# Slot logits in four copies, slot sums by column groups, and 128 bytes of padding in SBUF

## The chip, the cores and the metric

One core of a Trainium2 chip runs the whole program. The metric is the device time of one execution in microseconds. The engines are TensorE (PE, with its weight loads shown apart as PEld), VectorE (DVE), ScalarE (ACT), GpSimd (POOL) and SyncE (SP); DMAs are issued here from GpSimd (inputs and weights) and from SyncE (output).

## What is computed

Sliding-window attention over q, k, v of 8 batches, 8 heads, 576 positions and 64 dimensions, then a soft mixture of experts over its result x of 4608 tokens and 512 columns:

```python
scores = q @ k.T / 8; mask: 0 <= row - col < 64; attn = softmax(scores) @ v
x = attn.transpose(0, 2, 1, 3).reshape(4608, 512)
logits = x @ phi                              # 4608 x 32 slots, 8 experts x 4
d = exp(logits - max over tokens); d /= d.sum(0)
slot_input = (d.T @ x).reshape(8, 4, 512)
slot_out[e] = relu(slot_input[e] @ w1[e]) @ w2[e]     # 512 -> 1024 -> 512
c = exp(logits - max over slots); c /= c.sum(1)
out = c @ slot_out                            # 4608 x 512
```

The kernel takes no maximum away before either exp. One exp of the logits therefore serves both d and c; they differ in the sum that they are divided by.

## The kernel before

The attention goes through 16 units, each one batch and four heads (half of the heads). A unit has three steps j. A step transposes windows of v (stage_t2), makes scores for four windows of 64 queries (one window in the third step) and takes their exp on ScalarE to the tile pm (stage_s), transposes q, k or v of the next unit (stage_t1, copies to SBUF mostly by ScalarE), and multiplies the pm of the step before by v (stage_av, whose result goes to x_bp). The scores have one PSUM buffer, the tiles named tr, lt, pa and te share four.

GpSimd issues all loads in the order in which they are written, and that order is kept by hand (manual_schedule). issue_loads(u) loads q, k and v of unit u + 3 into three rotating buffers and one quarter of an expert's weights (load_w, 512 KB in SBUF); at unit 13 all that is left of the weights is issued in one go. The last weight tile, w2l, lies in a buffer of x_bp. All loads turn float32 in HBM into float16 in SBUF. At most eight of them are under way at a time: each waits for the one eight places ahead to have landed.

When both halves of a batch are through, six further pieces of work follow, one appended to each of the next six steps (the list todo): stage_xt(b, 0), (b, 1) and (b, 2) transpose x, chunk by chunk of 128 tokens (four chunks for even batches, five for odd ones, in which the last halves of two batches make up a chunk); stage_logit multiplies the transposed chunks by phi and takes the exp to ex, four copies side by side, with its sum over slots; stage_slot multiplies x by ex and adds up over batches in acc, a further product with ones giving the sum over tokens; stage_et transposes ex to ET. For the last batch all six follow the loop at once.

Then the experts: expert_h and expert_o work with four column groups of TensorE side by side, in each group a product with 32 slots. sop collects the result of all experts in one bank, slot_oa is its copy, and the last loop makes 36 products cp of ET with slot_oa, scales them by crcp and stores them by SyncE from the tiles ob, which lie in the buffers of w1s.

Of the kernel before, what the change touches and what calls it, by code (L numbers as in the profile page):

```python
# [8 lines left out]
FP32 = mybir.dt.float32  # L9
FP16 = mybir.dt.float16  # L10
AF = mybir.ActivationFunctionType
ALU = mybir.AluOpType
# [4 lines left out]
def kernel(  # L17
# [29 lines left out]
    pxt = ctx.enter_context(tc.tile_pool(name="pxt", bufs=3))  # L47
# [58 lines left out]
    ones = const.tile([128, 128], FP16, name="ones")  # L106
    nc.vector.memset(ones, 1.0)
# [15 lines left out]
    nc.gpsimd.dma_start(out=phi_sb, in_=moe_phi.rearrange("(c p) s -> p c s", p=128))  # L123

    ET = const.tile([128, 4 * B + B // 2, 128], FP16, name="ET")
    crcp = const.tile([128, B, 5], FP32, name="crcp")
    acc = const.tile([128, 5, NSLOT], FP32, name="acc")
# [122 lines left out]
    def stage_xt(b, part):  # L250
        xb = xbp[b // 2]
        ch = moe_chunks(b)[2 * part:2 * part + 2]
        if not ch:
            return
        tr = ps.tile([128, 8, 128], FP16, name="tr", tag="tr", bufs=4)
        for n, c in enumerate(ch):
            for kk in range(NHD):
                nc.tensor.transpose(tr[:, 4 * n + kk, :], xb[:, c, 128 * kk:128 * kk + 128], ident[:, :])  # L258
        xT = pxt.tile([128, 8, 128], FP16, name="xT", tag="xT")
        nc.vector.tensor_copy(out=xT[:, 0:4 * len(ch), :], in_=tr[:, 0:4 * len(ch), :])  # L260
        moe[b, part] = xT

    def stage_logit(b):
        ch = moe_chunks(b)
        lt = ps.tile([128, 5, NSLOT], FP32, name="lt", tag="tr", bufs=4)
        for n, c in enumerate(ch):
            xT = moe[b, n // 2]
            for kk in range(NHD):
                nc.tensor.matmul(lt[:, n, :], xT[:, 4 * (n % 2) + kk, :], phi_sb[:, kk, :],  # L269
                                 start=(kk == 0), stop=(kk == NHD - 1))  # L270
        nch = len(ch)
        ex = psm.tile([128, 5, 4, NSLOT], FP16, name="ex", tag="ex", bufs=2)
        nc.scalar.activation(ex[:, 0:nch, :, :],
                             lt[:, 0:nch, :].unsqueeze(2).broadcast_to([128, nch, 4, NSLOT]), AF.Exp)
        rs = psm.tile([128, 5], FP32, name="rs", tag="rs")
        nc.vector.reduce_sum(rs[:, 0:nch], ex[:, 0:nch, 0, :], axis=AXX)
# [3 lines left out]
    def stage_slot(b):  # L280
        ch = moe_chunks(b)
        xb = xbp[b // 2]
        ex = moe["ex", b]
        pa = ps.tile([128, 5, NSLOT], FP32, name="pa", tag="tr", bufs=4)
        for n, c in enumerate(ch):
            for dc in range(NHD + 1):
# [162 lines left out]
```

## Time and profile before

| what | value |
|---|---|
| median of 13 runs | 198.52 us (196.84 to 201.62) |
| the profiled execution | 197.24 us, of which the span from its first to its last instruction is 195.4 us |
| loads (q0) | 30.97 MB in SBUF, 94.2% of the span of 16 DMA engines |
| stores (q1) | 9.44 MB, 13.8% |
| TensorE | busy 142.1 us, 73% of the span |
| ScalarE, VectorE | busy 109.7 and 109.1 us, 56% each |
| HBM | 61.93 MB read, 9.44 MB written |

A row of a timeline has start, duration, engine, line, operation, out<-in and number of instructions, and in brackets the idle time before it and what ended it. A row of the chain has start, duration and what held the time. A row of a table of stages has the stretch, its length, busy time of PE, PEld, DVE, ACT and POOL (with number of instructions), the granted TensorE clock, the DMA engines' share and GB/s written. "issue" as a releaser means that nothing in the profile shows what the engine waited for. The profiled execution is one of the faster ones of the 13.

### The profile page before, as it was taken

To read this page: it belongs to the slowest core of one execution; us is meant where nothing else is said; L and a number is where in the kernel's file an instruction comes from. 1 tells how busy PE (TensorE), PEld (TensorE's weight loads), DVE (VectorE), ACT (ScalarE), POOL (GpSimd) and SP (SyncE) were. 2 spreads that over 40 slices of the span, in tenths; PEclk is the share of its full clock that TensorE was granted. 3 is DMA by queue.
4 is the path that set the end of the run, shared out by engine and by line. 5 is a ranking of instruction groups with operands and counts; after the bars stand their busy time and mean duration, and the time that the engine had idled before them with its cause. 6 is when DMAs were issued, how large, how long until landed. Compare 5 with 4: busy or idle time off the path is not lost.

```text
span 195.4 us, 7045 instructions
## 1 busy us (share of the span) xinstructions
PE 142.1 (73%) x3148; PEld 106.1 (54%) x3148; DVE 109.1 (56%) x268; ACT 109.7 (56%) x164; POOL 59.6 (31%) x89
## 2 busy tenths in 40 slices
PE   0699999878987879884988986898757774882000
PEld 0476777766766657763876865787644541220000
DVE  3026688657674757753885864578853113894000
ACT  2556876957566596765669566676311223893000
POOL 7953544434241424321442952232210000000000
PEclk9999999999999999999999998799985999798555
DMA  4999999999999999999699999999999991899995
GB/s 65 168 202 207 207 208 209 204 206 209 211 208 204 207 208 207 210 188 173 88 189 193 184 166 209 209 208 211 207 211 207 211 205 26 322 379 379 379 330 143
DMA packets 31310, 40.84 MB, mean 209 GB/s; under 512 B 2097, under 2 KB 22577, under 8 KB 31281
## 3 DMA queue, kind: packets, MB, share of 16 engines
q0 software_dynamic: 26384, 30.97, 94.2%
q1 hardware_dynamic: 4896, 9.44, 13.8%
q8 instruction: 24, 0.39, 0.7%
q14 instruction: 6, 0.04, 0.1%
HBM read 61.93 MB, written 9.44 MB: 365 GB/s over the span
## 4 chain that ended last, share of the span: by engine, by line
PE 43%; ACT 16%; DMA 13%; issue 10%; DVE 7%; POOL 1%; DVEq 0%; ACTq 0%; POOLq 0%
DMA w2l<-in_moe_w_dram 10%; PE tr L146 10%; PE tr L177 8%; ACT pm L200 7%; ACT kT L153 6%; PE sc L188 6%; PE sc L195 5%; PE av L223 4%; DVE ob L408 4%; DMA vn<-in_v_dram 3%; PE tr L258 2%; ACT qT L153 2%; PE cp L402 2%; PE pa L288 2%; PE lt L269 2%
## 5 line engine op out<-in xcount | busy, mean ns | idle before, releaser
L200 ACT ACTIVATE pm<-sc 128x1024 f16<-128x1024 f32 (+1 forms) x48 | 39.5, 822 | 38.6 <-PE sc L195 36.0
L178 DVE COPY vw<-tr 128x1024 f16<-128x1024 f16 (+1 forms) x48 | 26.5, 551 | 7.4 <-PE tr L177 7.3
L177 PE MATMUL tr<-ident,vT 128*128 128x128 f16 x288 | 24.8, 224 | 1.1 <-DVE rc L229 0.9
L153 ACT COPY qT<-tr 128x640 f16<-128x640 f16 (+1 forms) x32 | 21.9, 745 | 4.9 <-PE tr L146 4.9
L223 PE MATMUL av<-vw,pm 128*64 128x65 f16 x576 | 19.4, 197 | 4.2 <-issue 2.9
L231 DVE TENSOR_TENSOR x_bp<-av,rc 128x512 f16<-128x512 f32 x32 | 22.0, 688 | 0.8
L153 ACT COPY kT<-tr 128x640 f16<-128x640 f16 (+1 forms) x32 | 22.0, 761 | 0.2 <-PE tr L146 0.2
L188 PE MATMUL sc<-rep,hide 64*128 64x512 f16 (+1 forms) x96 | 20.8, 346 | 1.8 <-ACT pm L200 1.3
L195 PE MATMUL sc<-qT,kT 64*128 64x64 f16 x576 | 20.1, 193 | 1.9 <-issue 1.9
L177 PEld LDWEIGHTS <-vT 128*128 128x128 f16 x288 | 17.6, 100 | 4.7 <-issue 2.6
L195 PEld LDWEIGHTS <-kT 64*128 64x128 f16 x576 | 15.4, 96 | 7.3 <-issue 4.1
L223 PEld LDWEIGHTS <-pm 128*64 128x64 f16 x576 | 15.8, 112 | 6.6 <-issue 5.2
L61 POOL DMA_DIRECT2D vn<-in_v_dram x16 | 11.5, 717 | 21.1 <-PE av L223 16.8
L146 PE MATMUL tr<-ident,qn 128*64 128x128 f16 x288 | 12.3, 233 | 7.7 <-DMA qn<-in_q_dram 5.4
L151 DVE COPY vT<-tr 128x512 f16<-128x512 f16 x16 | 11.6, 726 | 10.9 <-PE tr L146 10.8
L61 POOL DMA_DIRECT2D qn<-in_q_dram x16 | 11.5, 717 | 18.5 <-PE av L223 10.4
L61 POOL DMA_DIRECT2D kn<-in_k_dram x16 | 11.5, 717 | 16.2 <-PE av L223 11.9
L81 POOL DMA_DIRECT2D w1s<-in_moe_w_dram x16 | 11.4, 718 | 13.4 <-DMA w1s<-in_moe_w_dram 9.9
L146 PE MATMUL tr<-ident,vn 128*64 128x128 f16 x288 | 13.4, 227 | 2.6 <-ACT kT L153 0.7
L146 PEld LDWEIGHTS <-qn 128*64 128x64 f16 x288 | 9.5, 117 | 8.6 <-DMA qn<-in_q_dram 5.4
L84 POOL DMA_DIRECT2D w2s<-in_moe_w_dram x14 | 10.6, 767 | 11.3 <-DMA w2s<-in_moe_w_dram 7.9
L408 DVE TENSOR_SCALAR ob<-cp,crcp 128x512 f32<-128x512 f32 x18 | 12.6, 747 | 1.3 <-PE cp L402 1.2
(63 smaller groups left out, 216.8 us busy)
## 6 DMA issues: line engine op xcount, KB each, us to landing
out_dram<-ob SPq DMA_DIRECT2D x18, 512.0 KB, 5.5
w1s<-in_moe_w_dram POOLq DMA_DIRECT2D x16, 512.0 KB, 13.6
w2s<-in_moe_w_dram POOLq DMA_DIRECT2D x14, 512.0 KB, 13.5
qn<-in_q_dram POOLq DMA_DIRECT2D x16, 288.0 KB, 10.6
kn<-in_k_dram POOLq DMA_DIRECT2D x16, 288.0 KB, 10.5
vn<-in_v_dram POOLq DMA_DIRECT2D x16, 288.0 KB, 9.9
w2l<-in_moe_w_dram POOLq DMA_DIRECT2D x2, 512.0 KB, 19.7
phi_sb<-in_moe_phi_dram POOLq DMA_DIRECT2D x1, 32.0 KB, 7.2
```

The costliest lines, as they stand in the source:

```text
L61: nc.gpsimd.dma_start(out=t, in_=src[b, 4 * half:4 * half + 4].rearrange("(x h) (g t) d -> (h g) x (t d)", x=2, h=2, t=T))
L146: nc.tensor.transpose(tr[64 * x:64 * x + 64, j, :], src[:, x, 64 * (t0 + j):64 * (t0 + j) + 64], ident[:, :])
L151: nc.vector.tensor_copy(out=o, in_=i)
L153: nc.scalar.copy(out=o, in_=i)
L177: nc.tensor.transpose(tr[:, 2 * w + h, :], st["vT"][:, h, 64 * i:64 * i + 128], ident[:, :])
L178: nc.vector.tensor_copy(out=st["vw"][:, wins[0]:wins[0] + n, :, 0:64], in_=tr[:, 0:2 * n, :].rearrange("p (w h) (x d) -> p w (h x) d", h=2 ...
L188: nc.tensor.matmul(sc[:, x, 0:128 * n], hide[64 * x:64 * x + 64, :], rep[64 * x:64 * x + 64, 0:2 * n, :], start=True, stop=False, skip_gro ...
L195: nc.tensor.matmul(sc[:, x, o:o + 64], st["kT"][64 * x:64 * x + 64, h, 64 * i:64 * i + 128], st["qT"][64 * x:64 * x + 64, h, 64 * i:64 * i ...
L200: nc.scalar.activation(pm[:, :, 0:2 * n, :], sc[:, :, 0:128 * n].rearrange("p x (w q) -> p x w q", q=64), AF.Exp, scale=scale)
L223: nc.tensor.matmul(av[r0:r0 + 64, kk, 65 * (w // 2):65 * (w // 2) + 65], pm[:, x, h * n + w, :], st["vw"][:, i, 2 * h + x, 0:65], start=Tr ...
L231: nc.vector.tensor_tensor(out=xb[:, c0:c0 + 2, 256 * half:256 * half + 256].rearrange("p c (k d) -> p k c d", d=64), in0=avv[:, :, :, 0:64 ...
L408: nc.vector.tensor_scalar(out=ob[:, g, :], in0=cp[:, :], scalar1=cr, scalar2=None, op0=ALU.mult)
```

## The change

Logits are made the other way round: phi, copied four times side by side (phi4), is the weight, and up to 512 tokens stream through, so that lt has slots on partitions, in four copies, and its exp is ET at once; ScalarE's instruction also writes the sum over tokens to esum. A fifth chunk takes four products of its own (l8) and an exp of its own. The new stage_ex multiplies ET by a part of the identity matrix, which gives ex with tokens on partitions; ScalarE copies it, VectorE takes the sum over slots. stage_slot takes ex as the weight, 32 columns in one of four column groups, and streams the 512 columns of x. Its four partial sums lie in four groups of partitions of pa; acc is now 128 x 512. After the loop acc is scaled by one over the sum over tokens (dinv) and sel4, a stack of four identity matrices, adds the four groups and transposes at once (si). The six pieces of work are now xt, xt, xt, logit, ex, slot. issue_loads takes two weight quarters in units 2, 5, 8 and 11. The pool of xT has one buffer of 4 KB and one of 1 KB, and a tile of 128 bytes (gap), which nothing uses, stands behind it in SBUF: the tiles w1s, w2s and ob start at 105056 and onward in steps of 8192 before, 104448 after (96 and 0 bytes past a multiple of 512), qn, kn and vn at 96 and 0 past a multiple of 256. TensorE's program has 5826 rows after, 6298 before.

```diff
@@ -44,7 +44,9 @@
     ppm = ctx.enter_context(tc.tile_pool(name="ppm", bufs=2))
     psm = ctx.enter_context(tc.tile_pool(name="psm", bufs=4))
     pxb = ctx.enter_context(tc.tile_pool(name="pxb", bufs=2))
-    pxt = ctx.enter_context(tc.tile_pool(name="pxt", bufs=3))
+    pxt = ctx.enter_context(tc.tile_pool(name="pxt", bufs=1))
+    gap = ctx.enter_context(tc.tile_pool(name="gap", bufs=1))
+    gap.tile([128, 64], FP16, name="gap")
     pw1 = ctx.enter_context(tc.tile_pool(name="pw1", bufs=8))
     pw2 = ctx.enter_context(tc.tile_pool(name="pw2", bufs=7))
     pet = ctx.enter_context(tc.tile_pool(name="pet", bufs=2))
@@ -103,8 +105,10 @@
         nc.vector.tensor_copy(
             out=rep[64 * h:64 * h + 64, :, :],
             in_=ident[64 * h:64 * h + 64, 64 * h:64 * h + 64].unsqueeze(1).broadcast_to([64, 8, 64]))
-    ones = const.tile([128, 128], FP16, name="ones")
-    nc.vector.memset(ones, 1.0)
+
+    sel4 = const.tile([128, NSLOT], FP16, name="sel4")
+    with nc.allow_low_precision("sums of 0 and 1"):
+        nc.vector.reduce_sum(sel4, ident.rearrange("p (g s) -> p s g", s=NSLOT), axis=AXX)
     kTs, vTs, vws, hTs = [], [], [], []
     for n in range(2):
         kt = const.tile([128, 2, 64 + S], FP16, name=f"kT{n}")
@@ -121,10 +125,13 @@
         vws.append(vw)
     phi_sb = const.tile([128, NHD, NSLOT], FP16, name="phi_sb")
     nc.gpsimd.dma_start(out=phi_sb, in_=moe_phi.rearrange("(c p) s -> p c s", p=128))
+    phi4 = const.tile([128, NHD, 4, NSLOT], FP16, name="phi4")
+    nc.vector.tensor_copy(out=phi4, in_=phi_sb.unsqueeze(2).broadcast_to([128, NHD, 4, NSLOT]))
 
     ET = const.tile([128, 4 * B + B // 2, 128], FP16, name="ET")
     crcp = const.tile([128, B, 5], FP32, name="crcp")
-    acc = const.tile([128, 5, NSLOT], FP32, name="acc")
+    acc = const.tile([128, D], FP32, name="acc")
+    esum = const.tile([128, B + B // 2], FP32, name="esum")
     slot_inT = const.tile([128, NHD, NSLOT], FP16, name="slot_inT")
     slot_oa = const.tile([128, D], FP16, name="slot_oa")
     for n in range(2):
@@ -252,56 +259,66 @@
         ch = moe_chunks(b)[2 * part:2 * part + 2]
         if not ch:
             return
+        nch = len(ch)
+        if part == 0:
+            moe[b] = pxt.tile([128, NHD, 4, 128], FP16, name="xT", tag="xT")
         tr = ps.tile([128, 8, 128], FP16, name="tr", tag="tr", bufs=4)
+        for kk in range(NHD):
+            for n, c in enumerate(ch):
+                nc.tensor.transpose(tr[:, nch * kk + n, :], xb[:, c, 128 * kk:128 * kk + 128], ident[:, :])
+        if part < 2:
+            nc.vector.tensor_copy(out=moe[b][:, :, 2 * part:2 * part + 2, :],
+                                  in_=tr[:, :, :].rearrange("p (k n) q -> p k n q", n=2))
+        else:
+            moe[b, 8] = pxt.tile([128, NHD, 128], FP16, name="xT8", tag="xT8")
+            nc.vector.tensor_copy(out=moe[b, 8], in_=tr[:, 0:4, :])
+
+    def stage_logit(b):
+
+        lt = ps.tile([128, 512], FP32, name="lt", tag="tr", bufs=4)
+        for kk in range(NHD):
+            nc.tensor.matmul(lt[:, :], phi4[:, kk].rearrange("p r s -> p (r s)"), moe[b][:, kk],
+                             start=(kk == 0), stop=(kk == NHD - 1))
+        nc.scalar.activation(ET[:, 4 * b:4 * b + 4, :], lt[:, :].rearrange("p (c q) -> p c q", q=128),
+                             AF.Exp, accum_out=esum[:, b:b + 1])
+        if b % 2:
+            l8 = ps.tile([128, 128], FP32, name="l8", tag="tr", bufs=4)
+            for kk in range(NHD):
+                nc.tensor.matmul(l8[:, :], phi4[:, kk].rearrange("p r s -> p (r s)"), moe[b, 8][:, kk],
+                                 start=(kk == 0), stop=(kk == NHD - 1))
+            nc.scalar.activation(ET[:, 4 * B + b // 2, :], l8[:, :], AF.Exp,
+                                 accum_out=esum[:, B + b // 2:B + b // 2 + 1])
+
+    def et_chunks(b):
+        return [4 * b + n for n in range(4)] + ([4 * B + b // 2] if b % 2 else [])
+
+    def stage_ex(b):
+
+        ch = et_chunks(b)
+        nch = len(ch)
+        te = ps.tile([128, 5, NSLOT], FP32, name="te", tag="tr", bufs=4)
         for n, c in enumerate(ch):
-            for kk in range(NHD):
-                nc.tensor.transpose(tr[:, 4 * n + kk, :], xb[:, c, 128 * kk:128 * kk + 128], ident[:, :])
-        xT = pxt.tile([128, 8, 128], FP16, name="xT", tag="xT")
-        nc.vector.tensor_copy(out=xT[:, 0:4 * len(ch), :], in_=tr[:, 0:4 * len(ch), :])
-        moe[b, part] = xT
-
-    def stage_logit(b):
-        ch = moe_chunks(b)
-        lt = ps.tile([128, 5, NSLOT], FP32, name="lt", tag="tr", bufs=4)
-        for n, c in enumerate(ch):
-            xT = moe[b, n // 2]
-            for kk in range(NHD):
-                nc.tensor.matmul(lt[:, n, :], xT[:, 4 * (n % 2) + kk, :], phi_sb[:, kk, :],
-                                 start=(kk == 0), stop=(kk == NHD - 1))
-        nch = len(ch)
-        ex = psm.tile([128, 5, 4, NSLOT], FP16, name="ex", tag="ex", bufs=2)
-        nc.scalar.activation(ex[:, 0:nch, :, :],
-                             lt[:, 0:nch, :].unsqueeze(2).broadcast_to([128, nch, 4, NSLOT]), AF.Exp)
+            nc.tensor.matmul(te[:, n, :], ET[:, c, :], ident[:, 0:NSLOT], start=True, stop=True)
+        ex = psm.tile([128, 5, NSLOT], FP16, name="ex", tag="ex", bufs=2)
+        nc.scalar.copy(out=ex[:, 0:nch, :], in_=te[:, 0:nch, :])
         rs = psm.tile([128, 5], FP32, name="rs", tag="rs")
-        nc.vector.reduce_sum(rs[:, 0:nch], ex[:, 0:nch, 0, :], axis=AXX)
+        nc.vector.reduce_sum(rs[:, 0:nch], te[:, 0:nch, :], axis=AXX)
         nc.vector.reciprocal(crcp[:, b, 0:nch], rs[:, 0:nch])
         moe["ex", b] = ex
 
     def stage_slot(b):
+
+        ex = moe["ex", b]
+        pa = ps.tile([128, D], FP32, name="pa", tag="tr", bufs=4)
         ch = moe_chunks(b)
-        xb = xbp[b // 2]
-        ex = moe["ex", b]
-        pa = ps.tile([128, 5, NSLOT], FP32, name="pa", tag="tr", bufs=4)
         for n, c in enumerate(ch):
-            for dc in range(NHD + 1):
-                lhs = xb[:, c, 128 * dc:128 * dc + 128] if dc < NHD else ones[:, :]
-                nc.tensor.matmul(pa[:, dc, :], lhs, ex[:, n, 0, :],
-                                 start=(n == 0 and dc == 0), stop=(n == len(ch) - 1 and dc == NHD),
-                                 skip_group_check=True)
+            g = n % 4
+            nc.tensor.matmul(pa[32 * g:32 * g + 32, :], ex[:, n, :], xbp[b // 2][:, c, :],
+                             start=(n < 4), stop=(n + 4 >= len(ch)), skip_group_check=True)
         if b == 0:
-            nc.vector.tensor_copy(out=acc[:, :, :], in_=pa[:, :, :])
-        else:
-            nc.vector.tensor_tensor(out=acc[:, :, :], in0=pa[:, :, :], in1=acc[:, :, :], op=ALU.add)
-
-    def stage_et(b):
-        ex = moe["ex", b]
-        nch = len(moe_chunks(b))
-        te = ps.tile([128, 8, 128], FP16, name="te", tag="tr", bufs=4)
-        for n in range(nch):
-            nc.tensor.transpose(te[:, n, :], ex[:, n].rearrange("p r s -> p (r s)"), ident[:, :])
-        nc.vector.tensor_copy(out=ET[:, 4 * b:4 * b + 4, :], in_=te[:, 0:4, :])
-        if nch > 4:
-            nc.vector.tensor_copy(out=ET[:, 4 * B + b // 2, :], in_=te[:, 4, :])
+            nc.vector.tensor_copy(out=acc[:, :], in_=pa[:, :])
+        else:
+            nc.vector.tensor_tensor(out=acc[:, :], in0=pa[:, :], in1=acc[:, :], op=ALU.add)
 
 
     nu = len(units)
@@ -310,7 +327,8 @@
     def issue_loads(u):
         if u + 3 < nu:
             load_unit(u + 3)
-            load_w(*w_order.pop(0))
+            for _ in range(2 if u % 3 == 2 else 1):
+                load_w(*w_order.pop(0))
 
     load_w(*w_order.pop(0))
     load_unit(2)
@@ -334,7 +352,7 @@
                 if pj == 2 and units[pu][1] == 1:
                     b = units[pu][0]
                     todo += [lambda b=b: stage_xt(b, 0), lambda b=b: stage_xt(b, 1), lambda b=b: stage_xt(b, 2),
-                             lambda b=b: stage_logit(b), lambda b=b: stage_slot(b), lambda b=b: stage_et(b)]
+                             lambda b=b: stage_logit(b), lambda b=b: stage_ex(b), lambda b=b: stage_slot(b)]
             pend = (u, j)
             if todo:
                 todo.pop(0)()
@@ -346,16 +364,23 @@
     stage_xt(b, 1)
     stage_xt(b, 2)
     stage_logit(b)
+    stage_ex(b)
     stage_slot(b)
-    stage_et(b)
+    dinv = const.tile([128, 2], FP32, name="dinv")
+    nc.vector.reduce_sum(dinv[:, 0:1], esum[:, :], axis=AXX)
+    nc.vector.reciprocal(dinv[:, 1:2], dinv[:, 0:1])
+
+    pa_sb = slot_oa
+    nc.scalar.activation(pa_sb[:, 0:256], acc[:, 0:256], AF.Copy, scale=dinv[:, 1:2])
+    nc.vector.tensor_scalar(out=pa_sb[:, 256:512], in0=acc[:, 256:512], scalar1=dinv[:, 1:2], scalar2=None, op0=ALU.mult)
     psum1.close()
 
 
     ps2 = ctx.enter_context(tc.tile_pool(name="ps2", bufs=2, space=bass.MemoryType.PSUM, reuse_waits="tile"))
-    dinv = const.tile([128, NSLOT], FP32, name="dinv")
-    nc.vector.reciprocal(dinv, acc[:, NHD, :])
-    nc.vector.tensor_tensor(out=slot_inT[:, :, :], in0=acc[:, 0:NHD, :],
-                            in1=dinv[:, :].unsqueeze(1).broadcast_to([128, NHD, NSLOT]), op=ALU.mult)
+    si = ps2.tile([128, NHD, NSLOT], FP32, name="si", tag="hp")
+    for dc in range(NHD):
+        nc.tensor.matmul(si[:, dc, :], pa_sb[:, 128 * dc:128 * dc + 128], sel4[:, :], start=True, stop=True)
+    nc.vector.tensor_copy(out=slot_inT, in_=si)
 
     sel = ident[:, :].rearrange("p (g s) -> p g s", s=NSLOT)
     sop = ps2.tile([128, D], FP32, name="sop", tag="sop", bufs=1)
```

Three places in the order of instructions.

GpSimd, the loads issued in unit 2 and the first of unit 3; before:

```order
L61 DMA qn<-in_q_dram 128x2x576
L61 DMA kn<-in_k_dram 128x2x576
L61 DMA vn<-in_v_dram 128x2x576
L84 DMA w2s<-in_moe_w_dram 128x4x512
L61 DMA qn<-in_q_dram 128x2x576
```

and after:

```order
L63 DMA qn<-in_q_dram 128x2x576
L63 DMA kn<-in_k_dram 128x2x576
L63 DMA vn<-in_v_dram 128x2x576
L86 DMA w2s<-in_moe_w_dram 128x4x512
L83 DMA w1s<-in_moe_w_dram 128x2x1024
L63 DMA qn<-in_q_dram 128x2x576
```

A second weight load stands ahead of the next unit's q.

ScalarE, the first two steps of a unit in which the logits of an odd batch (five chunks) are made; before:

```order
L153 COPY qT<-tr 128x128x4
L273 ACTIVATE ex<-lt 128x640
L200 ACTIVATE pm<-sc 128x1024
L153 COPY kT_116<-tr 128x2x64x5
L153 COPY kT_116<-tr 128x2x64x4
L200 ACTIVATE pm<-sc 128x2x128
```

and after:

```order
L160 COPY qT<-tr 128x128x4
L282 ACTIVATE ET,esum<-lt 128x512
L289 ACTIVATE ET,esum<-l_2253 128x128
L207 ACTIVATE pm<-sc 128x1024
L160 COPY kT_120<-tr 128x2x64x5
L160 COPY kT_120<-tr 128x2x64x4
L303 CAST ex<-te 128x160
L207 ACTIVATE pm<-sc 128x2x128
```

The exp is split in two and the copy of te comes ahead of the third step's exp.

VectorE, from the last transposes of x to the experts; before:

```order
L260 COPY xT<-tr 128x512
L276 TENSOR_REDUCE rs<-ex 128x5
L277 RECIPROCAL crcp<-rs 128x5
L294 TENSOR_TENSOR acc<-pa,acc 128x160
L302 COPY ET<-te 128x512
L304 COPY ET<-te 128x128
L356 RECIPROCAL dinv<-acc 128x32
L357 TENSOR_TENSOR slot_inT<-acc,dinv 128x128
```

and after:

```order
L274 COPY xT_3702<-tr 128x512
L370 TENSOR_REDUCE dinv<-esum 128x1
L371 RECIPROCAL dinv<-dinv 128x1
L305 TENSOR_REDUCE rs<-te 128x5
L306 RECIPROCAL crcp<-rs 128x5
L321 TENSOR_TENSOR acc<-pa,acc 128x512
L375 TENSOR_SCALAR slot_oa<-acc,dinv 128x256
L383 CAST slot_inT<-si 128x128
```

The copies to ET are gone, the sum is wider, and a scaling and the products si (on TensorE) lie between it and slot_inT.

## The prediction

> **What bounds the kernel now.** I read the page first (the slices, the DMA queues, the chain that ended last), then the DMA rate stage by stage, the end of the experts on TensorE, one step of the loop, and last the way from the loop to the experts and the stores.
>
> ```profile
> span 195.4 us, 7045 instructions
> ...
> q0 software_dynamic: 26384, 30.97, 94.2%
> q1 hardware_dynamic: 4896, 9.44, 13.8%
> q8 instruction: 24, 0.39, 0.7%
> ...
> PE 43%; ACT 16%; DMA 13%; issue 10%; DVE 7%; POOL 1%; DVEq 0%; ACTq 0%; POOLq 0%
> ```
>
> The loads (q0, 31 MB) and the stores (q1, 9.4 MB) share the 16 DMA engines, and the stores cannot start before the last expert is done. So the span is: loads and attention side by side, then the experts, then the stores. The stage view gives the DMA rate (last number of a row, GB/s) over three stretches.
>
> ```profile
> 15.00:85.00 70.00, 59.77 (x1532) 48.13 (x1530) 48.09 (x111) 48.84 (x73) 26.39 (x37) 1.00 1.20 207
> 85.00:118.00 33.00, 28.03 (x746) 23.23 (x740) 22.30 (x54) 23.51 (x35) 14.43 (x20) 1.00 1.07 169
> 118.00:161.00 43.00, 33.60 (x738) 24.60 (x735) 21.99 (x65) 18.22 (x30) 7.31 (x10) 0.88 1.18 208
> ```
>
> 207 to 208 GB/s is the full rate of the loads; between 85 and 118 us they ran at 169. The queue was empty there at times: 33 x (1 - 169/207) = 6.1 us of transfer were lost. The next rows say who was late (waiter, releaser, us in total, times, longest), and then how the experts ended.
>
> ```profile
> POOL vn L61 <- PE av L223: 16.8, 8, 4.0
> PE tr L146 <- DMA qn<-in_q_dram: 5.4, 1, 5.4
> ...
> 158.75 0.21 PE L374 MATMUL th<-ident,h_sb 128*128 128x16 f16 x2 [0.33 <-ACT h_sb L371]
> 158.89 0.40 PE L386 MATMUL sop<-w2s,hT 128*32 128x512 f16 x3
> ...
> 160.76 0.40 PE L386 MATMUL sop<-w2l,hT 128*32 128x512 f16 x4
> 163.09 0.40 PE L386 MATMUL sop<-w2l,hT 128*32 128x512 f16 x4 [1.93 <-DMA w2l<-in_moe_w_dram]
> ```
>
> GpSimd waits for TensorE to give input buffers back; TensorE waits for inputs only once, 5.4 us at the start. So the loop is a compute loop, and the DMA has a hole in it. At the end the two paths are nearly level: TensorE had everything else done at 161.16 (160.76 + 0.40) and waited 1.93 us for the last weights. That is all that a faster load can give, unless the compute path gets shorter too.
>
> **The loads.** Four more weight DMAs (512 KB, 2.5 us each at 208 GB/s) go into units 2, 5, 8 and 11, and as many leave the block at unit 13. Three of them, 7.5 us, are queued before or just as the hole opens, and it lost 6.1; so the last weights land about 163.0 - 6.1 = 157 and the wait of 1.93 us goes: **-1.9**. Less would be gained only if TensorE then came late for another reason, which stands in the terms below. The extra DMA stands in the queue behind its own unit's inputs and ahead of the next unit's, 2.5 us of delay. Since TensorE waits for inputs at the start alone, I cost that at nothing; its cover is three units of buffers, and without it each of the four would cost up to 2.5 us.
>
> **The loop.** Each step of a unit turns on ScalarE: exp of the scores (pm), copies of q or k, again exp. The rows are of one batch of five chunks: ScalarE and TensorE in order of time, the three removed TensorE stages from the chain, and three groups (busy us, mean ns) of small copies.
>
> ```profile
> 84.91 1.02 ACT L200 ACTIVATE pm<-sc 128x1024 f16<-128x1024 f32 x1 [2.62 <-PE sc L195]
> 85.83 1.37 ACT L153 COPY qT<-tr 128x640 f16<-128x640 f16 x2
> 87.04 0.73 ACT L273 ACTIVATE ex<-lt 128x640 f16<-128x640 f32 x1
> 87.62 1.06 ACT L200 ACTIVATE pm<-sc 128x1024 f16<-128x1024 f32 x1
> ...
> 86.77 0.40 PE L195 MATMUL sc<-qT,kT 64*128 64x64 f16 x16
> 91.35 0.19 PE L288 MATMUL pa<-ex,ones 128*128 128x32 f16 x1 [2.61 <-issue]
> ...
> 85.56 0.60 PE lt L269 x20
> 88.04 0.70 PE pa L288 x24
> 92.76 0.39 PE te L301 x5
> ...
> L371 ACT ACTIVATE h_sb<-hp 128x256 f16<-128x256 f32 x8 | 3.1, 384 | 12.0 <-PE hp L367 12.0
> L302 DVE COPY ET<-te 128x512 f16<-128x512 f16 x8 | 3.1, 392 | 0.4 <-PE te L301 0.4
> L304 DVE COPY ET<-te 128x128 f16<-128x128 f16 x4 | 0.9, 213 | 0.0
> ```
>
> Logit step: ScalarE runs without a gap from 84.91 to 87.62, while the scores that its next exp needs were ready at 87.17 (86.77 + 0.40): TensorE has 0.45 us of slack. A product of 512 columns in one column group follows the next by about 0.2 us: the bounds are 0.10 (four groups side by side, 0.40 for four) and 0.40 (one alone); I take 0.21. Four of them take 0.84 instead of 0.60 for 20 small ones; the ninth chunk adds four of 128 columns, 0.06 each: 1.08. The growth of 0.24 to 0.48 about uses up the slack, so ScalarE sets the step: its exp of 512 stays, and with odd batches a second exp of 128 columns comes, 0.25 (under the 0.38 of 256 columns, h_sb, and about the 0.21 that VectorE takes for 128): 3 x 0.25 in the loop, and 0.05 for the written sums in each, together +0.9 (0 to 2.5).
>
> Next step: the 20 to 25 slot products (0.70) make room for 4 or 5 products of 32 columns (0.03 each by 0.60/20, so 0.15), TensorE gets 0.5 us shorter; ScalarE takes a new copy of te of 128 or 160 columns, about 0.28. Before, this step was held by TensorE only in odd batches. So 4 x 0.2 longer and 3 x 0.3 shorter: about 0 (-1 to +2). Last step: te (0.39) against the new slot products, four groups at once 0.40 and a fifth 0.2; VectorE loses ET copies of 0.39 and 0.21 and takes a sum over 512 columns instead of 160: +0.1 x 7 = +0.7, of which half is in the shadow of the vT copies: +0.3 (0 to 1.5).
>
> ```profile
> PE pa L288 <- issue: 4.0, 2, 2.6
> PE av L223 <- issue: 2.9, 4, 0.8
> PE sc L195 <- issue: 1.9, 3, 0.9
> PE tr L146 <- issue: 1.7, 2, 1.3
> PE lt L269 <- issue: 1.6, 1, 1.6
> ```
>
> These stops have no releaser. There are 24 instruction transfers of 16 KB (q8), one for 256 rows of TensorE's program of 6298, and the stops come about one to a transfer: 12.1 us in these rows, 0.5 us each. The program shrinks to 5826 rows, 1.8 transfers fewer: **-0.9** (0 to -4.7, two stops of the longest sort). Against it, the hole in the loads is filled, and the transfers meet more traffic there: +0.4 for five of them (0 to +2.5). Loop in all: +0.9 + 0 + 0.3 - 0.9 + 0.4 = **+0.7** (-4 to +6).
>
> ```profile
> 14.67 0.69 DVE L178 COPY vw<-tr 128x1024 f16<-128x1024 f16 x1 [1.54 <-PE tr L177]
> ```
>
> At the start VectorE's copy to phi4 waits for the load of phi, ahead of the first copies to vw. VectorE is idle for 1.54 us before the second of them, which covers that: 0 (to 0.5).
>
> **From the last unit to the experts.**
>
> ```profile
> 143.32 0.29 PE L258 MATMUL tr<-ident,x_bp 128*128 128x128 f16 x2
> 144.43 0.70 ACT L273 ACTIVATE ex<-lt 128x640 f16<-128x640 f32 x1 [4.36 <-PE lt L269]
> 146.05 0.33 DVE L294 TENSOR_TENSOR acc<-pa,acc 128x160 f32<-128x160 f32 x1 [0.34 <-PE pa L288]
> 147.43 0.29 DVE L357 TENSOR_TENSOR slot_inT<-acc,dinv 128x128 f16<-128x128 f32 x1
> 147.78 1.19 PEld L367 LDWEIGHTS <-slot_inT 128*32 128x32 f16 x25 [1.50 <-DVE slot_inT L357]
> ...
> L231 DVE TENSOR_TENSOR x_bp<-av,rc 128x512 f16<-128x512 f32 x32 | 22.0, 688 | 0.8
> ```
>
> Here everything is on the path. New, from the last transposes (end 143.61): logits 0.84 + 0.24, 144.7; the first exp, 0.6, begins at 144.45 when the first four chunks are done, the second ends near 145.4; te and its copy 0.2 + 0.28, 146.0; slot products 0.6, 146.65; sum over 512 columns 0.69 (as L231), 147.4; scaling by halves 0.42, 147.85; four si products and their copy 0.3 + 0.29, 148.45 against 147.78: **+0.7** (0 to 1.5).
>
> **The stores.**
>
> ```profile
> GB/s 65 168 202 207 207 208 209 204 206 209 211 208 204 207 208 207 210 188 173 88 189 193 184 166 209 209 208 211 207 211 207 211 205 26 322 379 379 379 330 143
> ...
> L411 SPq DMA_DIRECT2D out_dram<-ob x16: 372/1225/1257, 165.9 to 183.8; - x16
> ```
>
> The stores run at a steady 379 GB/s: 9.44 MB take 24.9 us. The tiles they read (ob) start 96 bytes past a multiple of 256 in the SBUF of the program before, and exactly on one in the changed program; the inputs and weights move in the same way. No aligned transfer is in this trace. The bounds: nothing, as the stores stand; and the rate at which the loads read, twice 208 = 416 GB/s since four bytes are read for two written, which would take 22.7 us, -2.2. The issues, 1.225 us for 512 KB (428 GB/s), would not stop that. Nothing in the rows puts it nearer to one end, so I take the middle, **-1.1**. The Trainium skill (DMA: Bandwidth & Descriptors, How a descriptor splits into AXI transactions) says that a read which does not start on 256 bytes fetches from the boundary below and pays for those bytes; by that estimate 3 beats of 67, -1.1 us, the sum would be the same, and no run here shows it yet. For the loads the alignment costs or gives nothing, because TensorE is then the later one.
>
> **Sum.** -1.9 + 0.7 + 0.7 - 1.1 = -1.6 us. The profiled execution took 197.24 us (195.4 of span), 1.3 below the median of 198.52; the difference goes onto the median: 198.5 - 1.6 = **196.9 us**.
>
> **Rivals.** (1) Slower: the loop lengthens by what is added and gets nothing for what is taken, because slots and te lay in ScalarE's shadow. Per batch 0.24 or 0.48 of logits, 0.28 of copy, 0.25 of second exp (odd), 0.2 of slots: 4 x 0.72 + 3 x 1.21 = 6.5 in place of +0.7; 202.7. It decides from about +3.3 in the loop on (199.5). For it speaks the gapless ScalarE row, against it the TensorE rows of 0.70 and 2.61 in the same batch. (2) The padding does nothing: 198.0, no change. (3) The stores reach the loads' read rate and the stops nearly halve (-5 of 12): 196.9 - 1.1 - 4.1 = 191.7; half of it 194. (4) The loads do not end earlier (the hole moves): 163.1 stays, loop and tail are hidden behind it; -1.1 of stores alone, 197.4, at the edge of no change. (5) Switching the array between 128 and 32 columns costs a pause. The rows at 158.75 and 158.89 have such a switch: the 32-column product starts 0.14 after th, inside its 0.21, so none is seen. If it cost 0.2 twice a batch, 16 x 0.2 = 3.2: 200.1. The Trainium skill (TensorEngine Tiling (Array Packing), Key Properties) says that changing the mode drains TensorE; by that rule 200.1, by the row 196.9.
>
> **Chances.** Forecast (195.5 to 197.5) 0.37; (3) and parts of it 0.19; (2) with (4) and small misses of loop and tail, within 0.5%, 0.22; (1) 0.18; (5) 0.04. Half a percent, 1.0 us, is about what can be told from no change. Faster 0.56, same 0.22, slower 0.22. The range that leaves out 2 in 10, 193.6 to 199.9, cuts the far ends of (1), (3) and (5); the forecast's own is 195.5 to 198.
>
> **What would show it.** The last weights land near 157 and no sop product waits for them; the loads show no hole at 85 to 118; TensorE's stops without releaser fall a little; the step around the logits has no gap on ScalarE; hp starts 0.5 to 2 us later than 147.78; stores at 395 to 400 GB/s. It is wrong if the stores stay at 379, or if the unit with the logits takes over 0.5 us longer.

## The result, and the profile after

The changed kernel takes 189.83 us (median of 11 runs, 189.36 to 190.76), the kernel before in the same call 199.36 (48 runs, 195.99 to 202.32). The ratio is 0.961, 95% interval 0.958 to 0.964; it compares the fast executions of both kernels alone, 7.7 us apart, while the medians hold slower ones of the kernel before too and lie 9.5 us apart. The forecast was 196.9, its range 193.6 to 199.9: the sign was right, the size far off, and the time lies below the range. The nearest of the cases is rival (3), 191.7.

The profiled execution took 190.95 us. Its page, the parts that answer to those shown of before:

```profile
span 189.2 us, 6583 instructions
...
GB/s 61 153 201 208 207 208 206 207 210 209 207 207 207 208 208 208 206 208 207 208 207 208 209 206 209 207 212 207 210 209 208 209 167 22 264 403 406 408 378 140
...
q8 instruction: 23, 0.38, 0.7%
...
PE 38%; ACT 28%; DMA 14%; issue 7%; DVE 4%; POOL 1%; DVEq 0%; ACTq 0%; POOLq 0%
```

The span is 6.2 us shorter. The loads run at 206 to 212 GB/s without a hole, and the stores at 403 to 408 instead of 379. In the chain that ended last, ScalarE has gained (16% to 28%) about what TensorE, "issue" and VectorE have lost. TensorE's waits (waiter, releaser, us in total, times, longest) and the end of the experts:

```profile
PE tr L153 <- issue: 3.3, 5, 1.3
...
PE sop L411 <- DMA w2l<-in_moe_w_dram: 1.5, 1, 1.5
PE si L382 <- ACT slot_oa L374: 1.3, 1, 1.3
...
PE av L230 <- issue: 1.0, 2, 0.6
...
PE sc L195 <- issue: 0.3, 1, 0.3
PE tr L268 <- issue: 0.3, 1, 0.3
PE sc L202 <- issue: 0.2, 1, 0.2
```

```profile
133.82 0.39 ACT L207 ACTIVATE pm<-sc 128x256 f16<-128x256 f32 x1 [0.28 <-PE sc L202]
...
143.96 1.68 PE L392 MATMUL hp<-w1s,slot_inT 128*32 128x256 f16 x25 [0.38 <-DVE slot_inT L383]
...
156.83 0.40 PE L411 MATMUL sop<-w2l,hT 128*32 128x512 f16 x4
158.70 0.40 PE L411 MATMUL sop<-w2l,hT 128*32 128x512 f16 x4 [1.47 <-DMA w2l<-in_moe_w_dram]
```

The stops without a releaser ("issue") have fallen from 13.2 us to 5.0 (all of them up to 150 us, from the timelines). The last exp of the loop starts at 133.82 and before at this:

```profile
139.69 0.38 ACT L200 ACTIVATE pm<-sc 128x256 f16<-128x256 f32 x1 [1.32 <-PE sc L195]
```

So the span is made up as follows. The loop ends 5.9 us earlier. From its last exp to the first hp it takes 10.14 us (143.96 - 133.82) in place of 8.09 (147.78 - 139.69): +2.05. TensorE has everything but the last weights done at 157.23 (156.83 + 0.40), 3.9 earlier, and waits 1.5 for the last weights, less than before by 0.5. From the last sop product to the end it is 30.5 us (189.2 - 158.70) against 32.3: -1.8. In all 4.4 (163.09 - 158.70) + 1.8 = 6.2. That is less than the 7.7 us of the ratio, because the profiled execution of the changed kernel (190.95) is longer than all its other runs. The largest term is a loop that I had expected to get 0.7 us longer; that is what the experiments are mostly about.

### The profile page after: what moved, and what is told of

It reads as the page before. It is cut to its first block, busy times and chain, and to the rows that moved or that the text cites. A ratio compares the mean times of both kernels' runs of the same rounds, so it can differ in the third digit from the quotient of the medians.

```text
span 189.2 us, 6583 instructions
## 1 busy us (share of the span) xinstructions
PE 143.5 (76%) x2912; PEld 101.4 (54%) x2912; DVE 109.0 (58%) x259; ACT 112.4 (59%) x189; POOL 59.6 (32%) x89
## 4 chain that ended last, share of the span: by engine, by line
PE 38%; ACT 28%; DMA 14%; issue 7%; DVE 4%; POOL 1%; DVEq 0%; ACTq 0%; POOLq 0%
ACT pm L207 12%; DMA w2l<-in_moe_w_dram 10%; PE tr L153 7%; PE tr L184 7%; ACT kT L160 7%; ACT qT L160 5%; PE sc L195 5%; PE sc L202 5%; PE cp L427 4%; DMA kn<-in_k_dram 3%; PE av L230 3%; PE tr L268 3%; ACT ob L431 3%; PE pa L316 2%; PE lt L280 2%
## 5 line engine op out<-in xcount | busy, mean ns | idle before, releaser
L230 PE MATMUL av<-vw,pm 128*64 128x65 f16 x576 | 18.9, 196 | 2.1 <-DVE x_bp L238 1.1
L230 PEld LDWEIGHTS <-pm 128*64 128x64 f16 x576 | 15.1, 111 | 7.7 <-issue 6.8
L63 POOL DMA_DIRECT2D vn<-in_v_dram x16 | 11.5, 716 | 17.8 <-PE sc L202 6.2
L83 POOL DMA_DIRECT2D w1s<-in_moe_w_dram x16 | 11.3, 709 | 16.6 <-DMA w1s<-in_moe_w_dram 7.5
L63 POOL DMA_DIRECT2D qn<-in_q_dram x16 | 11.5, 720 | 13.9 <-PE tr L153 3.2
L153 PE MATMUL tr<-ident,kn 128*64 128x128 f16 x288 | 12.2, 228 | 3.5 <-DMA kn<-in_k_dram 2.0
L153 PE MATMUL tr<-ident,vn 128*64 128x128 f16 x288 | 12.8, 227 | 2.6 <-ACT kT L160 1.1
L236 DVE RECIPROCAL rc<-av 128x8 f32<-128x8 f32 x32 | 6.3, 196 | 14.0 <-PE av L230 14.0
```

The source lines that it names most:

```text
L63: nc.gpsimd.dma_start(out=t, in_=src[b, 4 * half:4 * half + 4].rearrange("(x h) (g t) d -> (h g) x (t d)", x=2, h=2, t=T))
L83: nc.gpsimd.dma_start(out=w1_t[e][:, c], in_=moe_w1[e].rearrange("(c p) f -> p c f", p=128)[:, c])
L153: nc.tensor.transpose(tr[64 * x:64 * x + 64, j, :], src[:, x, 64 * (t0 + j):64 * (t0 + j) + 64], ident[:, :])
L230: nc.tensor.matmul(av[r0:r0 + 64, kk, 65 * (w // 2):65 * (w // 2) + 65], pm[:, x, h * n + w, :], st["vw"][:, i, 2 * h + x, 0:65], start=Tr ...
```

## The experiments

The change was taken apart first: M for the new logits, ex and slot sums, A for the alignment of the tiles, W for the doubled weight loads in units 2, 5, 8 and 11. The explanations of the shorter loop, numbered as in the expectations: theory 1, M needs fewer rows of TensorE's program, and TensorE's stops fall by that; theory 2, aligned loads leave more room to the instruction transfers; theory 3, the new order of the loads (W) lets the stops fall; theory 4, which sharpens 1 and came after the first runs, TensorE's instructions arrive in blocks of 256 rows, the transfers of the blocks cannot follow each other faster than about every 6 us while the loads fill the DMA engines, and M has fewer rows for the same work; rival 5, the time that the products themselves take on TensorE sets the loop.

### One part alone

M alone: the changed kernel with one weight quarter to a unit, and a pad that puts the tiles back at 96 bytes past a multiple of 256.

```diff
+    gq = ctx.enter_context(tc.tile_pool(name="gq", bufs=1))
+    gq.tile([128, 48], FP16, name="gq")
...
-            for _ in range(2 if u % 3 == 2 else 1):
-                load_w(*w_order.pop(0))
+            load_w(*w_order.pop(0))
```

> The new logits, slot sums and te alone (M): one weight load a unit as before, and all input, weight and output tiles back at 96 bytes past a multiple of 256. Theory 1 (TensorE's program): the stops of TensorE without a releaser, 13 us before and 5 us after in PE's list of waits, fall because the new products need fewer program rows where the rows came fastest; then this run has about 5 us of stops, its last pm starts near 134 us (139.7 before) and it takes about 193 to 195 us. Theory 2 (alignment): the stops fall because instruction transfers share the DMA engines with loads that cost less when aligned; then this run keeps 12 to 14 us of stops, the last pm near 140, and 198 to 200 us. Stores at 379 GB/s by both.

Measured: 193.3 us, ratio 0.974 (0.968 to 0.979). Stops 4.5 us, last exp at 131.74, hp at 142.71. M alone shortens the loop by 8 us, as theory 1 has it.

A alone: the kernel before, with dinv written into acc and a 32-byte pad, so that w1s, w2s, ob, qn, kn and vn start 96 bytes lower.

> The program of before with all input, weight and output tiles moved 96 bytes down to multiples of 256 and 512 (A), nothing else. Theory 1: stops stay at 12 to 14 us, the last pm near 140 us, and only the stores change, 406 instead of 379 GB/s, -1.6 us: 196 to 197.5 us. Theory 2: stops near 5 us, the last pm near 134, stores at 406 GB/s: 191 to 193 us.

Measured: 197.87 us, ratio 0.998 (0.991 to 1.004). Its rates in 40 slices:

```profile
GB/s 67 148 201 207 207 211 203 207 207 209 211 206 206 207 209 205 201 162 175 148 148 153 198 173 200 212 206 210 207 212 206 212 207 78 155 407 408 408 401 151
```

The stores gain all that they can, 407 to 408 GB/s. The stops of TensorE stay at 11.3 us and the last exp at 140.79, and where the loads are full they read at the same 207 as before, so theory 2 falls. In this execution the last weights landed at 165.4 instead of 163.0, which ate the gain of the stores: the loads moved 205 GB/s from 15 to 85 us and 166 from 85 to 118, against 207 and 169 in the profiled execution before. Why it differs, these runs don't tell.

W alone: the kernel before with the loop from the diff in issue_loads.

```diff
-            load_w(*w_order.pop(0))
+            for _ in range(2 if u % 3 == 2 else 1):
+                load_w(*w_order.pop(0))
```

> The program of before with two weight loads in units 2, 5, 8 and 11 (W), nothing else. The hole in the loads between 85 and 118 us should fill and the last weights land near 157 us, so that the wait of 1.9 us before the last sop products goes: 196 to 198 us by theory 1, where the filled hole adds at most 2 us of stops. Theory 3 (order of loads): the stops fall by it to 5 us: 191 to 194 us.

Measured: 197.32 us, ratio 0.995 (0.988 to 1.003). Its last two stages, cut as in the prediction:

```profile
85.00:118.00 33.00, 28.78 (x680) 23.33 (x677) 20.99 (x52) 22.34 (x34) 13.74 (x19) 0.90 1.20 208
118.00:161.00 43.00, 34.49 (x768) 26.22 (x769) 23.14 (x67) 17.94 (x29) 6.57 (x9) 0.88 1.03 182
```

The hole is gone (208 instead of 169 GB/s), the last weights land at 157.48, 5.6 us earlier, and no product waits for them. Yet the kernel isn't measurably faster: the stops are still 11.5 us, the loop's last exp is at 141.08, 1.4 us later than before, hp at 149.18, and TensorE is now last. So theory 3 falls. (That the exp is later may be the clock: between 85 and 141 us the granted clock was 0.91 in this execution, 0.97 in the one before.)

M and W together, without A (the changed kernel with the pad gq):

> M and W together, without the alignment (all tiles 96 bytes past a multiple of 256). Theory 1: like the changed kernel but for the stores, which run at 379 instead of 406 GB/s: 1.6 to 2 us longer, 191 to 192 us, stops near 5 us. Theory 2: 196 to 198 us, stops 12 us or more.

Measured: 192.58 us, ratio 0.970 (0.964 to 0.977), stores at 374 to 381 GB/s. And M and A without W:

> The changed kernel with one weight quarter in every unit, as before (new stages and padding stay, the added weight loads go). Theory: loop as in the changed kernel or up to 2 us earlier (the run with the new stages alone had its last exp at 131.74 us against 133.82); a hole in the loads is back between 85 and 118 us, the last weights land at 158.5 to 161 and products wait for them 1.5 to 3 us; stores at 405 GB/s; 189.5 to 192 us, ratio 0.955 to 0.97. Rival (the added weight loads carry part of the gain by themselves): 192.5 or more, ratio above 0.97.

Measured: 190.99 us, ratio 0.963 (0.951 to 0.974), stores at 404 to 407 GB/s; the hole is back, but shallow (188 and 193 GB/s in two slices), the last weights land at 158.58 and a product waits 1.93 us for them. So W is worth nothing that can be told here, with M (189.83 against 190.99, overlapping intervals) or without; M carries most of the gain, and A about 2 us where M is there too: by the ratios 0.974 to 0.963 without W, where the intervals overlap, and 0.970 to 0.961 with it.

The gap tile alone left out, which puts w1s, w2s and ob at 128 past a multiple of 256 and leaves q, k and v aligned:

```diff
-    gap = ctx.enter_context(tc.tile_pool(name="gap", bufs=1))
-    gap.tile([128, 64], FP16, name="gap")
```

> The changed kernel without the tile gap: w1s, w2s and ob start 128 bytes past a multiple of 256 instead of on one; q, k and v stay on it. If the stores pay for any start off 256 bytes, they run at 379 GB/s and it takes 1.5 to 2 us longer, 191.5 to 192; if only the 32 bytes past a multiple of 64 cost, they run at 406 and the time stays at 190. The loop is the same by all theories.

Measured: 192.06 us, ratio 0.970 (0.962 to 0.978); the stores at 376 to 380 GB/s, as at 96 bytes.

### Why the loop is shorter: rows or work?

M takes 472 rows from TensorE's program and changes the work at the same time. Two kernels tell these apart. The first gives the changed kernel 480 rows back, with little work: 30 more products of 32 columns in each stage_ex, which the right ones then overwrite.

```diff
-        te = ps.tile([128, 5, NSLOT], FP32, name="te", tag="tr", bufs=4)
+        te = ps.tile([128, 16, NSLOT], FP32, name="te", tag="tr", bufs=4)
+        for _ in range(30):
+            nc.tensor.matmul(te[:, 0, :], ET[:, ch[0], :], ident[:, 0:NSLOT], start=True, stop=True)
```

> The changed kernel with 30 further products of 32 columns ahead of those of te in every batch; what they write is overwritten. TensorE's program has 6306 rows again (5826 in the changed kernel, 6298 before), and about 0.9 us more of products a batch. Theory 4 (instruction supply: a block of 256 rows comes once in 6.0 us while the DMA engines are full, and the loop cannot be faster than its blocks): 1.9 blocks more, up to 11 us, of which some is hidden where the loop is not held by blocks; last pm 139 to 144 us (133.8 in the changed kernel), 195 to 201 us. Rival 5 (TensorE's time): 0.9 us a batch on a TensorE that waits anyway; the same as wide_up within 1 us.

The second gives TensorE about as much work (four times 0.21 us for 30 times 0.03) in 64 rows over the whole program: four more products of 512 columns to a batch (te made as large as in the first).

```diff
+        for _ in range(4):
+            nc.tensor.matmul(te[:, :, :], ET[:, ch[0], :], rep[:, :, :], start=True, stop=True)
```

> The changed kernel with 4 further products of 512 columns at the same place: about the same 0.85 us of TensorE a batch as in rows_up, but 64 program rows more instead of 480 (5890). Theory 4: a quarter of a block; last pm 134 to 137 us, 190 to 192.5 us. Rival 5: as long as rows_up, 194 us or more.

Measured: 197.58 us with the 480 rows (ratio 0.994, 0.989 to 0.998) and 190.67 with the wide products (0.965, 0.953 to 0.977). TensorE's largest stops with the rows:

```profile
PE av L230 <- issue: 4.6, 4, 1.9
PE tr L153 <- issue: 2.7, 4, 1.2
PE sc L202 <- issue: 2.7, 3, 1.4
```

The stops add up to 13.3 us again (with the wide products 6.0), and the last exp is at 142.49, 8.7 us later than in the changed kernel (with the wide products 135.70, 1.9 later). The granted clock was 1.00 in all three loops. By the ratios, 480 rows take back 3.3 of the 3.9% that the change had gained; 64 rows with about the same work take back 0.4%, which the intervals don't tell from nothing. So rival 5 falls.

Where the stops stand says what paces them. In the timeline of TensorE, the first ones of the changed kernel and of the one with more rows:

```profile
31.36 0.21 PE L195 MATMUL sc<-rep,hide 64*128 64x128 f16 x1 [0.29 <-issue]
...
37.41 0.41 PE L153 MATMUL tr<-ident,kn 128*64 128x128 f16 x7 [0.16 <-issue]
...
43.36 0.27 PE L268 MATMUL tr<-ident,x_bp 128*128 128x128 f16 x2 [0.27 <-issue]
...
49.38 0.38 PE L202 MATMUL sc<-qT,kT 64*128 64x64 f16 x14 [0.25 <-issue]
```

```profile
32.17 0.21 PE L195 MATMUL sc<-rep,hide 64*128 64x128 f16 x1 [0.66 <-issue]
...
38.21 0.41 PE L153 MATMUL tr<-ident,kn 128*64 128x128 f16 x7 [0.15 <-issue]
...
44.22 0.20 PE L202 MATMUL sc<-qT,kT 64*128 64x64 f16 x2 [1.38 <-issue]
...
50.14 0.41 PE L230 MATMUL av<-vw,pm 128*64 128x65 f16 x14 [0.53 <-issue]
```

They come every 6.0 us in both, whatever the instructions are. The records of the instruction queue (q8) in the traces give the same, and in all thirteen kernels each stop ends 1.2 to 1.6 us after a transfer of that queue has ended. The distances in us from one transfer's start to the next one's, from the second transfer to the end of the loop:

```
changed kernel      6.5 6.0 6.1 5.8 6.1 7.4 6.1 6.1 6.1 6.1 5.9 6.0 6.0 6.3 5.9 6.1 6.0 6.0
with 480 more rows  6.7 6.0 6.0 6.0 6.2 5.9 6.1 6.1 5.9 6.0 6.0 6.0 6.1 6.0 6.9 5.9 5.8 6.0
```

### Is it the loads that set the 6 us?

If so, blocks should come faster when the DMA engines have room, and rows should then cost little. The weight loads were taken out of units 0 to 12 in three kernels (before, changed, changed with the 480 rows), so that all but one quarter are issued at unit 13 (shown for the changed kernel; in the kernel before it is the one line load_w). Their total means nothing, the weights then land near 184 us; the loop up to its last exp is what counts.

```diff
-            for _ in range(2 if u % 3 == 2 else 1):
-                load_w(*w_order.pop(0))
```

> The program of before, but no weights are loaded in units 0 to 12; all but the first quarter follow at unit 13. TensorE's program is unchanged (6298 rows). Theory 4: the DMA engines are not full in the loop, blocks come faster than one in 6.0 us, the stops of TensorE fall below 4 us and the last pm starts at 133 us or earlier (139.7 before). Rival: if the stops belonged to the shapes of the old products, they would stay at 11 to 13 us and the last pm at 139 to 141. The whole is longer by both, 215 to 225 us, because the weights come after the loop.

> The changed kernel with its weight loads taken out of units 0 to 12, so that all weights but one quarter are issued at unit 13, as the kernel before had it in the run with late weights (last exp of the loop at 129.30 us). The total is of no interest: the last weights land late, near 184 us, and 209 to 216 us are expected. Theory (instruction blocks behind the loads hold the loop): with the DMA engines mostly free there, the blocks come faster than they are used, and the 472 rows that the change takes away are worth little: last exp between 127 and 130.5 us, at most 2.3 us ahead of the kernel before with late weights (the part after 107 us, when loads are full again, may still give 1 to 2). Rival (the new stages need less work on the engines): the 5.9 us that the change gained in the loop stay, last exp near 123.4.

> The changed kernel with 30 more products of 32 columns in stage_ex of each batch (480 rows, overwritten by the products that follow) and with late weights. With full loads these rows brought the last exp 8.7 us later. Theory (blocks behind the loads): with the DMA engines mostly free most of that goes away, last exp at most 4 us later than that of the changed kernel with late weights; what is left is the 0.9 us of TensorE per batch (30 x 0.03) where it is not hidden, and the part after 107 us. Rival (the rows cost by their own time on TensorE or by breaking the order of the steps, whatever the DMA does): 7 to 9 us later again.

Measured: 219.24, 217.2 and 216.51 us in all (one run each). The changed kernel with late weights, its rates in 40 slices and, from its timeline, its last exp:

```profile
GB/s 81 170 203 206 206 206 204 139 128 119 113 120 125 123 133 114 119 115 124 159 208 209 210 209 209 208 209 209 209 207 211 205 211 197 10 391 402 408 402 153
```

```profile
128.73 0.38 ACT L207 ACTIVATE pm<-sc 128x256 f16<-128x256 f32 x1 [0.28 <-PE sc L202]
```

and the stops of all three, before, changed and with rows in this order:

```profile
PE av L223 <- issue: 2.1, 2, 1.9
...
PE sc L195 <- issue: 0.5, 1, 0.5
PE lt L269 <- issue: 0.5, 1, 0.5
```

```profile
PE tr L153 <- issue: 0.9, 2, 0.7
```

```profile
PE av L230 <- issue: 2.3, 1, 2.3
...
PE tr L184 <- issue: 0.3, 1, 0.3
```

| last exp of the loop | loads full | loads at about 125 GB/s from 40 to 105 us |
|---|---|---|
| before | 139.69 | 129.30 |
| changed | 133.82 | 128.73 |
| changed, 480 more rows | 142.49 | 131.16 |

With the loads at 125 to 129 GB/s (the DMA engines' share is then 0.91 to 0.92, against 1.20 beside full loads) the change is worth 0.6 us in the loop instead of 5.9, and the 480 rows cost 2.4 instead of 8.7. In these executions rows are dear only beside full loads. The distances of the transfers are 3.8 to 8.0 us there, and mostly 6 again once the loads are full after 107 us; nearly all stops that are left stand in that last part (two of 109.2 and 115.4 us in the kernel before, 2.34 us of its 3.1; 116.8 us in the one with rows). The granted clock between 107 and 130 us was 0.93 in the first and third kernel and 1.00 in the changed one, so up to 1.6 us of either small difference (23 x 0.07, an estimate) may be clock. Both rivals, that M saves work and that rows cost by their own time, fall: the one wanted the 5.9 us to stay, the other the 8.7. The kernel before agrees: its shortest distance, 3.5 us (88.9 to 92.4), stands where its loads had fallen to 184 GB/s, and with the hole filled (W alone) no distance is under 5.8.

## Why the prediction was wrong

**The stops (the step that failed).** The prediction had read the right lines: stops without releaser, about one to an instruction transfer, fewer rows after. It then priced "1.8 transfers fewer" at 0.5 us each, the visible 12.1 us over 24 transfers (its rows list 12 stops, 1.0 us each): -0.9. Measured: -8.1 us (13.16 to 5.04). What is visible is only the rest of a wait. With transfers 6.0 us apart, TensorE cannot go through 256 rows in less, and a stop is 6.0 us minus the time that it has work for in a block. A loop that is held this way is priced by the block: 472 rows are 1.84 blocks, up to 11 us. 8.1 of them came back; that in some places a block now holds more work than 6.0 us, as the distance of 7.4 us in the list suggests, would explain the rest, but was not tested. The prediction's own lower bound for this term, -4.7, came from visible stops as well, and was too near. The trace of before held the hint: its stops end at 60.6, 66.5, 72.5, 78.6 and 84.6 us, 6 us apart, and I had looked at their sums only.

**The steps of the loop.** Predicted +0.9 for the logits, 0 for the next step and +0.3 for the last. They can be read where no stop disturbs them, in the runs with late weights: the exps of one unit with an odd batch, before and changed.

```profile
78.38 1.02 ACT L200 ACTIVATE pm<-sc 128x1024 f16<-128x1024 f32 x1 [1.51 <-PE sc L195]
...
81.09 1.06 ACT L200 ACTIVATE pm<-sc 128x1024 f16<-128x1024 f32 x1
...
83.19 0.48 ACT L200 ACTIVATE pm<-sc 128x256 f16<-128x256 f32 x1
...
86.05 1.02 ACT L200 ACTIVATE pm<-sc 128x1024 f16<-128x1024 f32 x1 [1.73 <-PE sc L195]
```

```profile
78.76 1.02 ACT L207 ACTIVATE pm<-sc 128x1024 f16<-128x1024 f32 x1 [1.52 <-PE sc L202]
...
81.75 1.02 ACT L207 ACTIVATE pm<-sc 128x1024 f16<-128x1024 f32 x1
...
84.04 0.45 ACT L207 ACTIVATE pm<-sc 128x256 f16<-128x256 f32 x1
...
86.87 1.02 ACT L207 ACTIVATE pm<-sc 128x1024 f16<-128x1024 f32 x1 [1.72 <-PE sc L202]
```

Logits +0.28, next step +0.19, last -0.03; even batches give +0.13, +0.17 and -0.07 in the same way. Over three odd and four even batches: +1.4, +1.25 and -0.4, about +2.2 against the forecast's +1.2. This is rival (1)'s mechanism, at a third of its price. Together +2.2 - 8.1 = -5.9, and the loop came 5.9 earlier. That it fits so well is in part luck: between 118 and 128 us the granted clock was 0.83 before and 1.00 after, which could be up to 1.7 us of the 5.9 (10 x 0.17, an estimate) and stands in neither term. The +0.4 for filling the hole is in the stops.

**From the last unit to the experts.** Predicted +0.7 (0 to 1.5), measured +2.05. The rows:

```profile
138.30 1.02 PE L280 MATMUL lt<-xT,phi 128*128 128x512 f16 x4 [0.43 <-DVE xT L270]
...
139.85 0.19 ACT L282 ACTIVATION_READ_ACCUMULATOR ET<-lt 128x1 f32 x1
...
140.93 1.03 PE L316 MATMUL pa<-x_bp,ex 128*32 128x512 f16 x5 [0.38 <-ACT ex L303]
...
142.00 0.69 DVE L321 TENSOR_TENSOR acc<-pa,acc 128x512 f32<-128x512 f32 x1 [0.54 <-PE pa L316]
...
143.29 0.29 PE L382 MATMUL si<-sel,slot_oa 128*128 128x32 f16 x4 [1.33 <-ACT slot_oa L374]
```

The four products of lt took 1.02 for 0.84. The five of 512 columns in column groups took 1.03 where I had 0.6, but at a granted clock of 0.50 (140.7 to 142.5 us); in the kernel with the wide products, at a clock of 1.00, the same five took what I had:

```profile
143.55 0.60 PE L318 MATMUL pa<-x_bp,ex 128*32 128x512 f16 x5 [0.38 <-ACT ex L305]
```

So 0.43 of the +2.05 is the clock's, though the kernel before too had half clock in the last part of its stretch (144.7 to 151.6 us). The written sum is an instruction of its own, 0.19, where I had 0.05; and the way from one engine to the next (0.4 to 0.5 at each change in the brackets of TensorE and VectorE) was left out of my sum at the new stages (and that sum is 0.1 too long at te: 145.4 + 0.48 is 145.9). All the same it cost the total little, since the last weights were awaited.

**The loads.** The hole went, as predicted, and before the end the rate is full; but the last weights landed at 158.66 and not at 157. The last third of a megabyte comes in slowly, as the stages of the changed kernel show (last number GB/s):

```profile
152.00:154.00 2.00, 1.67 (x44) 1.23 (x48) 0.53 (x4) 0.38 (x1) 0.00 (x0) 1.00 1.23 208
154.00:156.00 2.00, 1.67 (x41) 0.86 (x30) 0.26 (x2) 0.48 (x2) 0.00 (x0) 1.00 0.72 117
156.00:158.00 2.00, 0.90 (x13) 0.32 (x10) 0.19 (x1) 0.28 (x1) 0.00 (x0) 1.00 0.32 53
```

The share of the DMA engines falls with the rate, from 1.23 to 0.32: they do not finish together. The wait of 1.93 us did not go but became 1.47, since TensorE came 3.9 us earlier. The run without W shows that the four moved loads did not matter: with M's shorter loop the hole is shallow anyway. In every kernel with M and early weights, and with W alone, the last weights land between 157.5 and 158.9 us, so a still earlier TensorE would gain little here: with M alone the loop ends 2.1 us earlier than in the changed kernel, and the wait for the last weights is 2.2 us instead of 1.5.

**The stores.** Predicted -1.1 as the middle of 0 and -2.2; measured -1.8, 403 to 408 GB/s, near the loads' read rate of 416. Choosing the middle between two bounds was the error here. By the Trainium skill (DMA: Bandwidth & Descriptors, How a descriptor splits into AXI transactions) a start off 256 bytes costs the bytes that are fetched in vain; the sign agrees with 374 to 381 GB/s at 96 and at 128 bytes, and the size is about 7% here instead of the 4.7% (3 beats on 64) that I had estimated from it. Rival (5), a pause at each change between 128 and 32 columns, shows nothing: the step with the slot products, which have these changes, got 0.03 to 0.07 us shorter, and five of them took the forecast 0.60 at full clock.

**Rival (3)** had both causes in one, the stores at the read rate and the stops nearly halved, and came within 2 us. It got 0.19 as a side case, because I priced the stops by what is seen of them, and its own 191.7 leaned on halving them without a reason for it; that it came near is luck.

## What to carry to other kernels

Where a long unrolled program runs beside full loads, look at where the stops without releaser stand: if they come at an even distance, the loop goes by instruction blocks, and its time is rows / 256 x that distance; then fewer, wider instructions pay even where they take no less engine time, and rows with no work in them cost. The engine time of the rows is not what counts: about the same TensorE work moved the last exp by 8.7 us in 480 rows and by 1.9 in 64. When a term of a sum has such a hidden floor, price it by its period, not by the rest that shows as a wait.

## What the runs showed of the hardware

An instruction block of 256 rows (16 KB) came no faster than about every 6 us (5.8 at the least) while the loads ran at 207 GB/s, and down to 3.8 us apart with the loads at about 125 GB/s; 480 nearly empty rows cost 8.7 us of loop in the one case and 2.4 in the other. The Trainium skill (Runtime: NRT & Kernel Launch, Instruction fetch mechanics) has the blocks of 256 instructions, and says that the crossing from one to the next is mostly hidden; these runs agree with the size and not with the hiding. That the transfers wait behind the load packets in the DMA engines is the natural reading, but only the dependence on the loads was shown, not the place where they wait; a program with the same rows and loads of another packet size was not tried. Stores from SBUF reached 401 to 409 GB/s in their full stretch from tiles that start on a multiple of 256 bytes and 374 to 381 from ones 96 or 128 past; the loads into the same tiles kept 207 either way. Five products of 512 columns in column groups took 0.60 us at a granted clock of 1.00 and 1.03 at 0.50, so a duration is read together with the clock of its stretch. An exp with a written sum was followed on ScalarE by an instruction of its own for the sum, 0.19 to 0.24 us.
